# The sums of phi(k) on VectorE instead of TensorE, and roundings of landed inputs later in the written order

## The chip, the core and the metric

One core of a Trainium2 chip runs the kernel. Its engines work in parallel and wait for each other by semaphores: TensorE (PE, products; PEld is its loading of weights), VectorE (DVE), ScalarE (ACT), GpSimd (POOL) and SyncE (SP). SP and POOL issue most of the DMA transfers. The metric is the device time in microseconds of one execution; the time before is the median of three runs.

## The reference

x is 2048 x 1024. Two branches are computed from it and mixed by a gate per row. Branch A is linear attention with 32 heads of 32, B a gated MLP with 3584 hidden columns:

```python
q, k, v = split(x @ wqkv)                       # 32 heads of 32
phi_q = concat(softmax(q @ w_phi), softmax(-(q @ w_phi)))     # 64 features; phi_k alike from k
kv = einsum("bhsf,bhsd->bhfd", phi_k, v)
z  = einsum("bhsf->bhf", phi_k)
o  = einsum("bhqf,bhfd->bhqd", phi_q, kv) / (einsum("bhqf,bhf->bhq", phi_q, z)[..., None] + 1e-6)
a  = o @ wo
b  = (gelu(x @ w_gate) * (x @ w_up)) @ w_down
g  = sigmoid((x * gate_w).sum(-1))
out = g * a + (1 - g) * b
```

## The kernel before

Everything is fp32. Products run on operands split in two parts: a rounded one ("high", line 117, on ScalarE, type fp32r) and the remainder ("low", line 120, on VectorE); three passes (high with high, high with low, low with high) make one product. Matrix products of large blocks use a scheme with seven products of half-size blocks instead of eight (`LEFT`, `RIGHT`, `INTO`), so a **unit** (one 256-column group of v, k, q, gate or up, over one half of the rows) is seven groups of twelve `MATMUL` of 128x512 on line 741, named after the bank they go to: a, p, c, a, a, c11 and b. Names in profile rows: `wgu`, `tyz` and `v` are the rounded weights of a unit, `x` and `s` the rounded parts of x and of its sums, `stage` the places where loads land, `h` results on their way out. In rows of the profile the buffer c11 reads as c.

Between groups, ScalarE copies one bank to another so that the next products accumulate on it: c<-b (line 758), c11<-a (line 762; read in rows as c<-a) and b<-a (line 769). A copy is short, but it stands in ScalarE's queue in the written order, with the roundings.

That order is not left to a scheduler. The body (lines 134 to 1318) is written under a manual schedule: **streams** (Python generators) each yield a request (engine, assumed length, when ready, due), and `run` picks, product by product, the next one to emit, keeping a clock of its own with assumed lengths (`PRODUCT` 2.73 us, `LAND` 5.0 us for a load, and so on). `step` emits a group of products and notes when it begins and ends on that clock; small products (**fillers**) are put in behind a group once their inputs are assumed to be there. On the chip each engine then works its queue strictly in the order that came out; where a landing is later than assumed, all behind it on that engine waits.

Stages: a first part with the folding of w_phi into the key and query weights (lines 517 and 949), the gates (line 920, one product with gate_w for each 128 rows of x, whose loads come from SP), then the units of v and k, with gate and up units among them. `features` works on the background for each of 32 pairs (half of rows, head group, half of the group): a transpose, softmax of k, rounding of phi(k) into `pts`, and then additions over row blocks on VectorE (line 1022) that leave a 128x128 block `z` in the tile `tails` (line 1025). `accumulate` puts in as a filler eight products phi(k)^T v (line 1037) and one product of `z` with a column of ones (line 1039), which sums over partitions. The 257 columns go by ScalarE (line 1049) and a POOL DMA that adds into `kv_parts` in HBM. `finish` reads them back, sums and writes `sums_of`, from which `attention` works for q. From 1665 us on a last stage makes the output (line 1439).

x changes twice under the running products: at `first_turn` the right operands go from the second half of the rows to the first, at `second_turn` back. `x_convert` rounds each landed piece (its loads are line 270). `weights` and `lower_weights` load and round the weights of a unit.

Of the kernel before, what the change touches and what calls it, by code (L numbers as in the profile page):

```python
# [8 lines left out]
F32 = mybir.dt.float32  # L9
# [22 lines left out]
def tile_gated_mix(ctx: ExitStack, tc: tile.TileContext, x, xT, wkT, wqT, wv, w_phi, wo,  # L32
# [15 lines left out]
    one = keep.tile([P, 1], F32, name="one")  # L48
# [8 lines left out]
    kv_parts = dram.tile([P, H // 2, 2 * P + 1], F32, name="kvp")  # L57
# [76 lines left out]
    with tc.tile_pool(name="xa", bufs=1) as xa, tc.tile_pool(name="fp", bufs=1) as fp, \  # L134
# [16 lines left out]
        INF, PRODUCT, SIGNAL, LAND, STORE = 10.0 ** 9, 2.73, 0.12, 5.0, 4.5  # L151
        busy, begins, ends = {VEC: 0.0, SCA: 0.0}, {}, {}
# [119 lines left out]
        def x_convert(s, half, part, landed):  # L272
            i, j, last, need = part
            b0, s = 2 * half, s.rearrange("p (a b) -> p a b", a=2)
            end = yield SCA, 1.1, lambda: max(value(landed), done(last - 1)), need - 1.5
# [8 lines left out]
            low(q[1], s, q[0])  # L284
            return end

        def pieces(t, half, s, which, free, then=lambda end: None):
# [41 lines left out]
        def weights(n, half, kind, m):  # L329
# [4 lines left out]
            end = yield SCA, 1.1, lambda: max(landed, done(t - 9)), t - 2.2  # L334
# [28 lines left out]
        def lower_weights(n, kind, m, ke, e, ko, o, end, sums):  # L363
# [16 lines left out]
            end = yield SCA, 0.65, lambda: max(landed, done(t + 4)), t + 9.5  # L380
# [120 lines left out]
        nc.vector.memset(one, 1.0)  # L501
# [282 lines left out]
        def step(j, operand, *args, **kw):  # L784

            begins[j] = max(begins[j], operand - SIGNAL)
            product(*args, **kw)
# [49 lines left out]
        def last_products(n, half):  # L837
# [7 lines left out]
            mm=g_at.rearrange("p c q -> p (c q)")[:, :32], st=g_at.rearrange("p c q -> p (c q)")[:, 32:],  # L845
            z=tails[:, P:]))]
# [125 lines left out]
        def features(p):  # L972
# [12 lines left out]
            while job:  # L985
# [33 lines left out]
                end = yield VEC, 1.15, end - SIGNAL, soon()  # L1019
# [10 lines left out]
        v_free, z_free = [0.0], [0.0]  # L1030

        def accumulate(half, pair, pts, blocks):

            def emit_products(end):
                po = misc()
                for b in range(8):
                    nc.tensor.matmul(po[:, :2 * P], blocks[:, b], pts[:, b].rearrange("p e q f -> p (e q f)"),  # L1037
                                     start=b == 0, stop=b == 7, skip_group_check=True)
                nc.tensor.matmul(po[:, 2 * P:2 * P + 1], places[0].parts["z"], one, start=True, stop=True,
                                 skip_group_check=True)  # L1040
                misc_free[0] = INF
                pts_free[0] = v_free[0] = z_free[0] = end
# [3 lines left out]
        def accumulated(half, pair, po, end):  # L1046
            end = yield SCA, 0.45, lambda end=end: max(end, hidden_free()), now[0] + 2
            own = hidden()[:, :2 * P + 1]
            nc.scalar.activation(own, po[:, :2 * P + 1], AF.Copy)
# [5 lines left out]
        def finish(p):  # L1055
            landed = yield SYN, LAND + 7.0, lambda: max(max(kept), place_free(), v_free[0], pts_free[0]), INF
            zs, z = p.small("mm", 32)[:, :16], tails[:, :64]
# [4 lines left out]
            for c, t in enumerate(chunks):  # L1062
                nc.sync.dma_start(t.rearrange("p (u n) -> p u n", n=2 * P), kv_parts[:, 4 * c:4 * c + 4, :2 * P])
# [16 lines left out]
            yield VEC, 0.8, end - SIGNAL, soon()  # L1080
            nc.vector.memset(z[:, 16:32], 0.0)
            nc.vector.tensor_copy(z[:, :16], zs)
            nc.vector.transpose(z[:, 32:], z[:, :32])
# [444 lines left out]
```

## Time and profile before

| | |
|---|---|
| time, median of 3 | 2359.07 us (2357.88 to 2360.53) |
| profiled execution | 2356.42 us, its span 2354.4 us |
| TensorE busy | 2327.5 us, 99% of the span |
| VectorE, ScalarE busy | 1789.0 us, 1113.3 us |
| granted TensorE clock, mean | 0.996 |
| DMA | 622.36 MB, mean 264 GB/s |

In rows of a timeline stand the start and the length in us, the engine, line, operation, tiles (out<-in), shape and count, and in brackets the idle time of that engine ahead of it and what ended it. Lengths of neighbouring products overlap, since they are pipelined: the distance of two starts is the time a group takes. Rows of groups have total busy us, mean ns of one, and the idle time ahead. Rows of waits have the total, the count and the longest. Rows of stretches have from:to, length, then busy us and count of each engine shown (PE alone, or PE, PEld, DVE, ACT and POOL), the granted clock as a share of full speed, the DMA share and GB/s.

### The profile page before, as it was taken

What the parts mean: (1) busy time and instruction counts of PE and PEld (TensorE: products, weight loads), DVE (VectorE), ACT (ScalarE), POOL (GpSimd) and SP (SyncE); (2) the same over time, 40 slices, a digit from 0 to 9 for tenths busy, and PEclk for the clock granted to TensorE, in tenths of its full rate; (3) what the DMA queues carried; (4) which work ended last, traced back from release to release, by engine and by line L of the source; (5) the groups of instructions that cost most, each with busy time, mean ns of one, the idle gap of its engine ahead of it and who ended that gap; (6) DMA issues with size and microseconds to landing.
All of it is one profiled execution on the core that took longest, in us unless ns stands there. A gap on an engine that the chain in (4) does not pass through costs nothing.

```text
span 2354.4 us, 29380 instructions
## 1 busy us (share of the span) xinstructions
PE 2327.5 (99%) x10472; PEld 1930.8 (82%) x10472; DVE 1789.0 (76%) x2335; ACT 1113.3 (47%) x1498; POOL 379.0 (16%) x646
## 2 busy tenths in 40 slices
PE   8999999999999999999999999999999999999999
PEld 7777887888888888878888888888888888888887
DVE  6665787888888878866988888887574868767773
ACT  6435444555555555544565655655433222323221
POOL 3211111121222112122232222222000000000000
PEclk9999999999999999999999999999999999999999
DMA  9987447898989888899888888887784767978774
GB/s 340 308 295 275 146 155 257 307 314 289 324 304 308 309 282 295 284 294 256 246 257 247 235 248 250 236 249 239 263 286 157 260 237 264 322 258 316 262 268 136
DMA packets 242210, 622.36 MB, mean 264 GB/s; under 512 B 34000, under 2 KB 73680, under 8 KB 226192
## 3 DMA queue, kind: packets, MB, share of 16 engines
q1 hardware_dynamic: 152960, 308.48, 40.7%
q0 software_dynamic: 87904, 311.75, 39.6%
q8 instruction: 83, 1.36, 0.2%
q14 instruction: 63, 0.52, 0.1%
q10 hardware_dynamic: 1200, 0.26, 0.1%
HBM read 413.80 MB, written 206.59 MB: 264 GB/s over the span
## 4 chain that ended last, share of the span: by engine, by line
PE 90%; DMA 4%; issue 2%; DVE 2%; SPq 1%; ACT 1%; POOL 0%; DVEq 0%; ACTq 0%; POOLq 0%
PE po L1439 29%; PE a L741 25%; PE c L741 17%; PE b L741 8%; PE p L741 8%; PE misc L1194 1%; PE misc L1037 1%; DMA stage<-wk 1%; DMA stage<-in_wv 1%; DMA xs<-x 1%; SPq L968 1%; PE misc L949 0%; DMA stage<-in_xT 0%; DMA x<-in_xT 0%; DMA wk<-wgu 0%
## 5 line engine op out<-in xcount | busy, mean ns | idle before, releaser
L1439 PE MATMUL po<-tw,wgu 128*128 128x512 f32 x1344 | 309.8, 389 | 0.0
L1439 PEld LDWEIGHTS po<-tw,wgu 128*128 128x128 f32 x1344 | 252.3, 188 | 52.3
L117 ACT ACTIVATE wgu<-stage 128x1024 fp32r<-128x1024 f32 x130 | 137.5, 1058 | 301.5 <-PE po L1439 226.7
L120 DVE TENSOR_TENSOR wgu<-stage,wgu 128x1024 fp32r<-128x1024 f32 x130 | 158.8, 1221 | 131.1 <-ACT wgu L117 131.1
L741 PE MATMUL c<-x,tyz 128*128 128x512 f32 x948 | 234.5, 397 | 12.8 <-ACT c L758 10.9
L741 PE MATMUL c<-x,wgu 128*128 128x512 f32 x948 | 229.6, 391 | 0.3 <-ACT c L762 0.3
L741 PE MATMUL a<-s,tyz 128*128 128x512 f32 x948 | 229.6, 391 | 0.2 <-DVE tyz L120 0.2
L741 PE MATMUL b<-s,tyz 128*128 128x512 f32 x948 | 228.8, 390 | 0.0
L741 PE MATMUL a<-x,wgu 128*128 128x512 f32 x948 | 228.5, 390 | 0.3 <-DVE h L725 0.3
L741 PE MATMUL a<-s,v 128*128 128x512 f32 x948 | 228.8, 390 | 0.0
L741 PE MATMUL p<-s,tyz 128*128 128x512 f32 x948 | 228.2, 389 | 0.0
L741 PEld LDWEIGHTS c<-x,tyz 128*128 128x128 f32 x948 | 181.2, 192 | 53.7 <-ACT c L758 13.2
L741 PEld LDWEIGHTS a<-x,wgu 128*128 128x128 f32 x948 | 177.6, 188 | 37.8 <-DVE h L725 0.7
L741 PEld LDWEIGHTS a<-s,tyz 128*128 128x128 f32 x948 | 177.5, 188 | 37.7 <-DVE tyz L120 0.9
L741 PEld LDWEIGHTS p<-s,tyz 128*128 128x128 f32 x948 | 177.7, 188 | 36.7
L741 PEld LDWEIGHTS a<-s,v 128*128 128x128 f32 x948 | 177.4, 188 | 37.0 <-DMA v<-ru13v 0.3
L741 PEld LDWEIGHTS c<-x,wgu 128*128 128x128 f32 x948 | 177.0, 188 | 37.3 <-ACT c L762 0.7
L741 PEld LDWEIGHTS b<-s,tyz 128*128 128x128 f32 x948 | 177.4, 188 | 36.7
L1439 PE MATMUL po<-tw,wl 128*128 128x512 f32 x672 | 156.9, 389 | 0.0
L1439 PE MATMUL po<-tyz,wgu 128*128 128x512 f32 x672 | 155.2, 389 | 0.0
L1439 PEld LDWEIGHTS po<-tyz,wgu 128*128 128x128 f32 x672 | 126.2, 188 | 26.2
L1439 PEld LDWEIGHTS po<-tw,wl 128*128 128x128 f32 x672 | 126.2, 188 | 26.2
(440 smaller groups left out, 3556.2 us busy)
## 6 DMA issues: line engine op xcount, KB each, us to landing
stage<-lm SPq DMA_DIRECT2D x98, 512.0 KB, 3.7
sr<-in_w_down SPq DMA_DIRECT2D x84, 512.0 KB, 6.0
sl<-lm SPq DMA_DIRECT2D x70, 512.0 KB, 4.5
lm<-h POOLq DMA_DIRECT2D x112, 256.0 KB, 4.7
stage<-in_w_gate SPq DMA_DIRECT2D x28, 512.0 KB, 5.4
stage<-in_w_up SPq DMA_DIRECT2D x28, 512.0 KB, 6.5
stage<-la SPq DMA_DIRECT2D x28, 512.0 KB, 5.2
sr<-in_wo SPq DMA_DIRECT2D x20, 512.0 KB, 6.2
```

Of the source, the lines that this page charges most:

```text
L117: nc.scalar.activation(dst, src, AF.Copy)
L120: nc.vector.tensor_tensor(dst, src, dst_h.bitcast(F32), OP.subtract)
L741: nc.tensor.matmul(dst, w[:, h, 4 * part + kc, :], xq[:, e, kc, :], start=first and kc == 0 and i == 0, stop=kc == 3 and i == 2, skip_grou ...
L968: nc.sync.dma_start(into[64 * j + 32 * i:64 * j + 32 * i + 32, n], heads[k][half][g][j][64 * w:64 * w + 64, 256 * i:256 * i + 256] .rearra ...
L1037: nc.tensor.matmul(po[:, :2 * P], blocks[:, b], pts[:, b].rearrange("p e q f -> p (e q f)"), start=b == 0, stop=b == 7, skip_group_check=True)
L1194: nc.tensor.matmul(po[s], kbs[:, s].rearrange("p a b -> p (a b)"), pts[:, q, s, :], start=q == 0, stop=q == 1)
L1439: nc.tensor.matmul(ps[c], ls[:, a, m, c * P:(c + 1) * P], rs[:, e, m], start=opens and m == 0 and j == 0, stop=closes and m == 1 and j == 2)
```

## The change

1. **z.** The product with ones goes, and with it the column 257 of `kv_parts`. `features` puts the accumulation in as a filler before the additions, and after them transposes the 128x128 block in its 32x32 squares on VectorE and reduces it over 32 columns into four numbers per partition, kept in `tails` (`z_sums`). `finish` adds up the two halves of rows and the partition groups by additions and shifting copies on VectorE, transposes once, and starts the four DMAs of z to `sums_of` ahead of the summing of kv, not behind it. The fetch of z from HBM goes.
2. **Roundings.** `soft` lets the planner assume that a landed input is ready for its rounding up to 2 us later (`SPARE`) than the load lands, if its due time allows, from `first_turn` on. It holds for pieces of x, for the even weights of a unit and for its `v`.
3. **Other assumed times.** `step` takes the end of the roundings of its x pieces into account (`x_ready`); loads of x pieces have a due time; the landing of wqT is assumed 4 us later; VectorE's lengths are taken 2% shorter from some way behind `first_turn` and 5% (was 3%) behind `second_turn`; the filler of an accumulation is assumed 0.9 us long (was 1.1).

```diff
+        SPARE = 2.0
+        def soft(landed, due):
+            at = begins.get(now[0], INF)
+            if now[0] < first_turn:
+                return landed
+            return max(landed, min(landed + SPARE, (at if at < INF else 0.0) + (due - 1.5 - now[0]) * PRODUCT))
...
-            return request[1] * (0.97 if request[0] == VEC and now[0] > second_turn + 14 else 1.0) + (1.3 if len(request) > 4 and request[4] != table[0] else 0.0)
+            return request[1] * (1.0 if request[0] != VEC else 0.95 if now[0] > second_turn + 14 else 0.98 if now[0] > first_turn + 70 else 1.0) + (1.3 if len(request) > 4 and request[4] != table[0] else 0.0)
...
-            end = yield SCA, 1.1, lambda: max(value(landed), done(last - 1)), need - 1.5
+            end = yield SCA, 1.1, lambda: max(soft(landed, need - 1.5), done(last - 1)), need - 1.5
...
+        def x_ready(n, half, i):
+            if 7 * n < first_turn:
+                return 0.0
+            assert len(x_made[half, i]) == 2
+            return max(x_made[half, i])
...
-                landed = yield SYN, LAND + 3.5, lambda: max(begun(part[2] - 5), value(free)), INF
+                landed = yield SYN, LAND + 3.5, lambda: max(begun(part[2] - 5), value(free)), part[3] - 5
...
-            end = yield SCA, 1.1, lambda: max(landed, done(t - 9)), t - 2.2
+            end = yield SCA, 1.1, lambda: max(soft(landed, t - 2.2), done(t - 9)), t - 2.2
...
-            end = yield SCA, 0.65, lambda: max(landed, done(t + 4)), t + 9.5
+            end = yield SCA, 0.65, lambda: max(soft(landed, t + 9.5), done(t + 4)), t + 9.5
...
-            begins[j] = max(begins[j], operand - SIGNAL)
+            begins[j] = max(begins[j], operand - SIGNAL, x_ready(n, half, x) - SIGNAL)
...
-                landed = yield SYN, LAND + 2.0, lambda: free[g % 2], INF
+                landed = yield SYN, LAND + 6.0, lambda: free[g % 2], INF
                 nc.sync.dma_start(s, wqT[g])
...
-                end = yield VEC, 1.15, end - SIGNAL, soon()
+                fillers.append((lambda end=end: max(end, misc_free[0]), accumulate(half, 2 * g + w, pts, blocks), 0.9))
+                yield VEC, 1.15, end - SIGNAL, soon()
                 half_sums = p.wide[0].rearrange("p (q n) -> p q n", q=4)
...
-                end = yield VEC, 0.3, lambda: max(end, z_free[0]), soon()
-                z_free[0] = INF
-                nc.vector.tensor_tensor(p.parts["z"].rearrange("p (q f) -> p q f", q=4), half_sums[:, :, :32],
+                p.free = yield VEC, 0.7, 0.0, soon()
+                z, zt = p.wide[0][:, P:2 * P], p.wide[0][:, 3 * P:4 * P]
+                nc.vector.tensor_tensor(z.rearrange("p (q f) -> p q f", q=4), half_sums[:, :, :32],
                                         half_sums[:, :, 32:64], OP.add)
-                p.free = end
-                fillers.append((lambda end=end: max(end, misc_free[0]), accumulate(half, 2 * g + w, pts, blocks), 1.1))
+                nc.vector.transpose(zt, z)
+                nc.vector.tensor_reduce(z_sums[:, half, :, 2 * g + w], zt.rearrange("p (q t) -> p q t", q=4), AX.X, OP.add)
...
-                nc.tensor.matmul(po[:, 2 * P:2 * P + 1], places[0].parts["z"], one, start=True, stop=True,
-                                 skip_group_check=True)
...
-            nc.sync.dma_start(zs, kv_parts[:, :, 2 * P])
             soon = lambda: now[0] + 3
+            yield VEC, 1.1, 0.0, soon()
+            nc.vector.tensor_tensor(z, z, other, OP.add)
+            for at in (32, 96):
+                nc.vector.tensor_copy(other[at - 32:at], z[at:at + 32])
+            nc.vector.tensor_tensor(z[:96], z[:96], other[:96], OP.add)
+            nc.vector.tensor_copy(other[:32], z[64:96])
+            nc.vector.tensor_tensor(z[:32], z[:32], other[:32], OP.add)
+            nc.vector.transpose(other[:32], z[:32])
+            for q in range(4):
+                nc.gpsimd.dma_start(sums_of[32 * q:32 * q + 32, 1].rearrange("b u d -> u b d"),
+                                    other[16 * (q % 2):16 * (q % 2) + 16, 32 * (q // 2):32 * (q // 2) + 32]
+                                    .unsqueeze(1).to_broadcast([16, 32, 32]))
```

What the written order makes of it is seen in three places. In the changed file the lines have other numbers: the rounding is L116, c<-b L772, c<-a L776, b<-a L783, the gelu L711, the exponentials L1020, the products L755, the folds of the query weights L962, the remainder L119 and the copies of kv's sums L1103.

ScalarE, the first gate unit behind the key and value units, from the copy b<-a to the copy c<-b. Before:

```order
L769 ACTIVATE b<-a 128x512
L117 ACTIVATE tyz<-stage 128x1024
L117 ACTIVATE f<-x_374 128x16x32
L1049 ACTIVATE h<-misc 128x257
L780 ACTIVATE x_374<-p 128x512
L117 ACTIVATE v<-stage 128x512
L697 ACT_TABLE_LOAD
L697 ACTIVATE x_374<-c_349 128x512
L1007 ACT_TABLE_LOAD
L1007 ACTIVATE x_374<-x_374 128x512 x2
L758 ACTIVATE c<-b 128x512
L117 ACTIVATE tyz<-stage 128x1024
```

Now:

```order
L783 ACTIVATE b<-a 128x512
L116 ACTIVATE tyz<-stage 128x1024
L794 ACTIVATE x_373<-p 128x512
L1062 ACTIVATE h<-misc 128x256
L711 ACT_TABLE_LOAD
L711 ACTIVATE x_373<-c_348 128x512
L116 ACTIVATE v<-stage 128x512
L772 ACTIVATE c<-b 128x512
L116 ACTIVATE tyz<-stage 128x1024
L116 ACTIVATE f<-x_373 128x16x32
L116 ACTIVATE wgu<-stage 128x1024
```

The rounding of `v`, which waits for a load, was followed by a table load, the gelu, another table load and two exponentials before c<-b; now the gelu stands ahead of `v`, and c<-b directly behind it.

TensorE, the first four folds of the query weights (`misc<-f,raw`) among the groups of two units. Before:

```order
L741 MATMUL c<-x_398,tyz 128x512 x12
L949 MATMUL misc<-f,raw 128x128 x8
L741 MATMUL a<-s_340,tyz 128x512 x12
L741 MATMUL a<-s_342,v 128x512 x12
L949 MATMUL misc<-f,raw 128x128 x8
L741 MATMUL c_349<-x_396,wgu 128x512 x12
L741 MATMUL b<-s_341,tyz 128x512 x12
L741 MATMUL a<-x_395,wgu 128x512 x12
L741 MATMUL p<-s_339,tyz 128x512 x12
```

Now (the same stretch and the unit behind it, to the fourth fold):

```order
L755 MATMUL a<-s_339,tyz 128x512 x12
L962 MATMUL misc<-f,raw 128x128 x8
L755 MATMUL a<-s_341,v 128x512 x12
L755 MATMUL c_348<-x_394,wgu 128x512 x12
L755 MATMUL b<-s_340,tyz 128x512 x12
L962 MATMUL misc<-f,raw 128x128 x8
...
L962 MATMUL misc<-f,raw 128x128 x8
L755 MATMUL a<-s_341,v 128x512 x12
L755 MATMUL c_348<-x_394,wgu 128x512 x12
L755 MATMUL b<-s_340,tyz 128x512 x12
L755 MATMUL a<-x_393,wgu 128x512 x12
L962 MATMUL misc<-f,raw 128x128 x8
```

Before, the second fold of a unit stood right behind a<-s,v, in both units; now it stands two and then three groups later.

ScalarE, the second turn of x (`x01` is the piece that the product c<-x,tyz reads). Before:

```order
L723 ACTIVATE h_8221<-c11_349 128x512
L117 ACTIVATE x01_8226<-stage_8148 128x1024
L117 ACTIVATE x01_8226<-stage_8167 128x1024
L758 ACTIVATE c_351<-b_350 128x512
L762 ACTIVATE c11_349<-a_8219 128x512
```

Now:

```order
L737 ACTIVATE h_8294<-c11_348 128x512
L116 ACTIVATE x01_8299<-stage_8236 128x1024
L772 ACTIVATE c_350<-b_349 128x512
L116 ACTIVATE x01_8299<-stage_8253 128x1024
L776 ACTIVATE c11_348<-a_8292 128x512
```

One of the two roundings of `x01` moved behind c<-b. The two copies of kv's sums (`f<-x00 32x1024`, L1079, now L1103) moved up by more than a unit, from behind these rows to the c<-b before.

More of the change, by code (lines that the diff above doesn't have):

```diff
@@ L47, in tile_gated_mix @@
     pair_mask = keep.tile([P, 2, 32], F32, name="pair_mask")
-    one = keep.tile([P, 1], F32, name="one")
     logit = keep.tile([P, S // P], F32, name="logit")
@@ L56, in tile_gated_mix @@
     wq_fold = [dram.tile([P, KC * P], F32, name=f"wq{g}") for g in range(NG)]
-    kv_parts = dram.tile([P, H // 2, 2 * P + 1], F32, name="kvp")
+    kv_parts = dram.tile([P, H // 2, 2 * P], F32, name="kvp")
     xb = {}
@@ L284, in x_convert @@
             low(q[1], s, q[0])
+            x_made[half, i].append(end)
             return end
+        x_made = {(half, i): [] for half in range(2) for i in range(7)}
+        def x_ready(n, half, i):
[3 more added lines that the diff above has]
+            return max(x_made[half, i])
         def pieces(t, half, s, which, free, then=lambda end: None):
@@ L500, in tile_gated_mix @@
             nc.vector.memset(pair_mask[32 * j:32 * j + 32, j % 2, :], 1.0)
-        nc.vector.memset(one, 1.0)
         bd = fp.tile([P, NG, 4, 32], F32, tag="v", name="bd", bufs=1)
@@ L782, in banks, with step @@
                         yield from result(kind, half, m, 1, 0, c11, None, lambda: done(t + 5), t + 8)
-        def step(j, operand, *args, **kw):
-            begins[j] = max(begins[j], operand - SIGNAL)
-            product(*args, **kw)
+        def step(j, operand, n, dst, right, part, x, half, first=False):
+            begins[j] = max(begins[j], operand - SIGNAL, x_ready(n, half, x) - SIGNAL)
+            product(n, dst, right, part, x, half, first)
             ends[j] = begins[j] + PRODUCT
@@ L844, in tile_gated_mix @@
         places = [Place(work[:, 2048:3072], dict(
-            mm=g_at.rearrange("p c q -> p (c q)")[:, :32], st=g_at.rearrange("p c q -> p (c q)")[:, 32:],
-            z=tails[:, P:]))]
+            mm=g_at.rearrange("p c q -> p (c q)")[:, :32], st=g_at.rearrange("p c q -> p (c q)")[:, 32:]))]
         misc_free, other_free, SOON = [0.0], [0.0], 2
@@ L1038, in emit_products @@
                                      start=b == 0, stop=b == 7, skip_group_check=True)
-                nc.tensor.matmul(po[:, 2 * P:2 * P + 1], places[0].parts["z"], one, start=True, stop=True,
-                                 skip_group_check=True)
                 misc_free[0] = INF
-                pts_free[0] = v_free[0] = z_free[0] = end
+                pts_free[0] = v_free[0] = end
                 start(accumulated(half, pair, po, end + 0.25))
@@ L1047, in accumulated @@
             end = yield SCA, 0.45, lambda end=end: max(end, hidden_free()), now[0] + 2
-            own = hidden()[:, :2 * P + 1]
-            nc.scalar.activation(own, po[:, :2 * P + 1], AF.Copy)
+            own = hidden()[:, :2 * P]
+            nc.scalar.activation(own, po[:, :2 * P], AF.Copy)
             nc.gpsimd.dma_start(kv_parts[:, pair], own, **({} if half else dict(accum_op=OP.add)))
@@ L1056, in finish @@
             landed = yield SYN, LAND + 7.0, lambda: max(max(kept), place_free(), v_free[0], pts_free[0]), INF
-            zs, z = p.small("mm", 32)[:, :16], tails[:, :64]
+            z, other = tails[:, :64], tails[:, 64:P]
             p.second(new_f(F32)[:, :1024])
@@ L1079, in finish @@
                 nc.scalar.activation(p.wide[1][rows[h]], p.wide[0][64 * h + 32:64 * h + 64], AF.Copy)
[L1080 to L1083, printed above, removed]
-            for q in range(4):
-                nc.gpsimd.dma_start(sums_of[32 * q:32 * q + 32, 1].rearrange("b u d -> u b d"),
-                                    z[32 * q:32 * q + 16, 32:].unsqueeze(1).to_broadcast([16, 32, 32]))
             end = yield VEC, 2.5, moved, soon()
```

5 lines of the change are left out of this document (3 added, 2 removed).

## The prediction

> **What bounds the kernel now.** I read the page's busy line, then whom TensorE waited for, then its busy time and granted clock by stage, then the timeline at each wait.
>
> ```profile
> span 2354.4 us, 29380 instructions
> PE 2327.5 (99%) x10472; PEld 1930.8 (82%) x10472; DVE 1789.0 (76%) x2335; ACT 1113.3 (47%) x1498; POOL 379.0 (16%) x646
> ...
> PE c L741 <- ACT c L758: 10.9, 5, 3.9
> PE misc L949 <- issue: 3.0, 1, 3.0
> ...
> PE c L741 <- DVE x L120: 1.2, 1, 1.2
> PE c L741 <- ACT x L117: 0.7, 1, 0.7
> ...
> 60.00:150.00 90.00, 82.86 (x390) 1.00 0.87 297
> 150.00:235.00 85.00, 83.07 (x393) 0.96 0.83 286
> 403.00:1037.00 634.00, 634.00 (x2916) 528.87 (x2915) 525.26 (x672) 352.50 (x489) 124.68 (x220) 1.00 0.88 301
> 1049.00:1665.00 616.00, 616.00 (x2719) 1.00 0.84 244
> ```
> TensorE (PE) sets the time: from 403 to 1037 us and from 1049 to 1665 us its busy time equals the stretch. So two things count: products that leave its queue, and its few waits, which lie before 1049 us. In the waits a row gives the sum, the number of waits and the longest; in the stretches the third figure from the end is the granted clock.
>
> **Term 1, the z products.** Each of the 32 accumulations (eight products of line 1037) is followed by a one-column fp32 product (L1039, two passes), which goes.
>
> ```profile
> 275.74 1.12 PE L1037 MATMUL misc<-pts,f 128*128 128x256 f32 x8
> 276.69 0.28 PE L1039 MATMUL misc<-one,tails 128*128 128x1 f32 x2
> 276.83 3.03 PE L741 MATMUL a<-s,v 128*128 128x512 f32 x12
> 279.70 2.88 PE L741 MATMUL c<-x,wgu 128*128 128x512 f32 x12
> 282.42 2.88 PE L741 MATMUL b<-s,tyz 128*128 128x512 f32 x12
> ```
> By starts, a plain group of twelve takes 282.42 - 279.70 = 2.72 us; z with the group behind it takes 279.70 - 276.69 = 3.01. Each z costs 0.29 us, of which 0.14 is its own and 0.15 a slower group behind it. 32 x 0.29 = 9.3 us, on an engine without a pause there. If the slower group came from the eight products and stayed, 32 x 0.14 = 4.5. I take -9.3.
>
> **Term 2, the wait at 392 us.**
>
> ```profile
> 389.26 2.88 PE L741 MATMUL p<-s,tyz 128*128 128x512 f32 x12
> 396.04 5.49 PE L741 MATMUL c<-x,tyz 128*128 128x512 f32 x12 [3.90 <-ACT c L758]
> 401.33 3.19 PE L741 MATMUL a<-s,tyz 128*128 128x512 f32 x12
> 404.35 2.88 PE L741 MATMUL a<-s,v 128*128 128x512 f32 x12
> ...
> 390.50 0.63 ACT L117 ACTIVATE v<-stage 128x512 fp32r<-128x512 f32 x1 [6.43 <-DMA stage<-in_w_gate]
> 391.15 1.28 ACT L697 ACT_TABLE_LOAD   x1
> 392.45 0.60 ACT L697 ACTIVATE x<-c 128x512 f32<-128x512 f32 x1
> 393.06 1.28 ACT L1007 ACT_TABLE_LOAD   x1
> 394.36 1.15 ACT L1007 ACTIVATE x<-x 128x512 f32<-128x512 f32 x2
> 395.41 0.58 ACT L758 ACTIVATE c<-b 128x512 f32<-128x512 f32 x1
> ```
> The copy c<-b that the product needs stands on ScalarE behind the rounding of v, whose load landed late, and behind two table loads, a gelu and two exponentials. 404.35 - 389.26 = 15.09 us for three groups instead of 8.16: 6.9 us lost, of which 3.9 is idle and the rest half clock. In the changed order table load and gelu stand ahead of v, and c<-b directly behind it. Landing as late, the copy would begin at 391.15 and end at 391.73, before the 391.98 at which the product is due. -6.9; if the load comes 3.9 us later still, 0.
>
> **Term 3, the wait at 1040 us.**
>
> ```profile
> 1037.88 2.88 PE L741 MATMUL p<-s,tyz 128*128 128x512 f32 x12
> 1043.91 4.44 PE L741 MATMUL c<-x,tyz 128*128 128x512 f32 x12 [3.14 <-ACT c L758]
> 1048.19 2.89 PE L741 MATMUL a<-s,tyz 128*128 128x512 f32 x12
> ...
> 1042.32 1.06 ACT L117 ACTIVATE x<-stage 128x1024 fp32r<-128x1024 f32 x1 [3.94 <-DMA stage<-in_xT]
> 1043.28 0.58 ACT L758 ACTIVATE c<-b 128x512 f32<-128x512 f32 x1
> ```
> 1048.19 - 1037.88 = 10.31 for two groups instead of 5.44: 4.9 us. Two roundings of x stand ahead of c<-b; now one does. But the second half of the same product reads the second x: landing at 1042.32 as before, rounded and its remainder taken, it would still hold the product for over 2 us. What may bring it sooner is SP's queue: the four kvp reads of the sum (2 MB), which stood right ahead of these two x loads, now have ten other loads between, and the fetch of z in 4-byte pieces goes. Ends 0 and -4.9; I take the middle, -2.5.
>
> **Term 4, the wait at 146 us.**
>
> ```profile
> 149.45 3.56 PE L949 MATMUL misc<-f,raw 128*128 128x128 f32 x16 [2.97 <-issue]
> ...
> 147.91 1.22 DVE L920 SCALAR_TENSOR_TENSOR x<-x 128x1024 f32<-128x1024 f32 x1 [2.29 <-DMA x<-in_x]
> ...
> 149.06 0.28 DVE L459 TENSOR_TENSOR f<-f 128x128 f32<-128x128 f32 x1
> ...
> 153.70 1.22 DVE L920 SCALAR_TENSOR_TENSOR x<-x 128x1024 f32<-128x1024 f32 x1
> ...
> 231.00:236.00 5.00, 5.00 (x16) 3.95 (x15) 2.94 (x4) 1.72 (x2) 0.00 (x0) 0.66 0.98 298
> ```
> The product of line 949 needs the small mask product of L459, which stands on VectorE (DVE) behind a gate product waiting for its x rows. 2.97 us idle, and then half clock: after the shorter waits at 228 us (0.7 and 1.2 idle) the five us from 231 ran at a mean 0.66, 1.7 us lost, and I price this one alike: 4.7. In the changed order this fourth fold stands three groups later: due at 149.45 - 2.97 + 8.16 = 154.6. On DVE its mask now follows the ninth gate product instead of the seventh. At the old pace the ninth began at 153.70; with the product, a half remainder (0.6) and the mask (0.3) that makes 155.8, a wait of some 1.2 us instead of 2.97 and its half clock. I take -3.5; ends -4.7 and 0, the latter if the x rows come 2 us later still.
>
> The Trainium skill (TensorE: Matmul & The Clock Gate, HAM oscillation) tells of no harm from PE gaps under about 3.4 us. By it only term 2 holds half clock, and terms 3 and 4 shrink by 0.9 and 1.7. The trace differs: the 0.66 followed idles of 0.7 and 1.2 us.
>
> **Term 5, what is late next.**
>
> ```profile
> 136.20 3.04 PE L741 MATMUL c<-x,tyz 128*128 128x512 f32 x12 [2.05 <-ACT c L758]
> L120 DVE TENSOR_TENSOR wgu<-stage,wgu 128x1024 fp32r<-128x1024 f32 x130 | 158.8, 1221 | 131.1 <-ACT wgu L117 131.1
> ```
> Here c<-b stands behind a rounding of wgu that waits for its load, and still does: ahead of x's first turn the softening does not act. That load stands on SP's queue behind the fourth load of gate rows, which needs the buffer of the second gate product; that product now stands behind one remainder (1.2 us) and two half-size sums (as much again). Up to 2.5 us later, or nothing if the load lands sooner for less traffic: +1.0, ends -3.7 (2.05 and half clock gone) and +2.5. The waits at 228 us (1.9 idle, 1.7 by clock) have roundings of x behind one of wgu before and after: 0, ends -3.6 and +2.
>
> For the new order as a whole I add one new wait of the size seen at 228 us, 0.7 idle and 1.7 by clock: +2.4. Its likeliest place is the second turn, where the two copies of the attention sums, which need the kvp reads, eight additions and a transpose, now stand on ScalarE ahead of an h<-c and a c<-b; they stood behind both. Ends 0 and +7, the price of term 2. More would be at odds with the rows: the old order had no wait in 403 to 1037 and 1049 to 1665, 1250 us, and in the new one a rounding of wgu stands between copy b<-a and copy c<-b in 6 of 79 places instead of 30.
>
> **Hidden parts.** z's sum on DVE:
>
> ```profile
> L988 DVE STREAM_TRANSPOSE x<-x 128x1024 f32<-128x1024 f32 x32 | 39.8, 1245 | 1.1
> L1083 DVE STREAM_TRANSPOSE tails<-tails 128x32 f32<-128x32 f32 x1 | 0.2, 213 | 0.0
> L995 DVE TENSOR_REDUCE g_at<-x 128x16 f32<-128x512 f32 x32 | 21.7, 678 | 0.1
> ```
> A transpose of 128 columns lies between 213 and 1245 ns, in proportion near 0.31 us; the reduction of 128 below 0.68, near 0.28. 32 x 0.59 = 19 us more on DVE, which idles 109 of the 634 us to 1037: nothing on PE's path; uncovered, 19. The accumulation is now queued for PE ahead of these sums, so it does not wait for them. At the end ten small operations replace three and the four stores of sums on POOL's queue come earlier; PE has products from the other stream there: 0, at most 2 if DVE is late. The spills shrink from 257 to 256 columns: 0. ScalarE issues the same copies.
>
> **Sum.** -9.3 - 6.9 - 2.5 - 3.5 + 1.0 + 2.4 = -18.8. It is made against the profiled execution, 2356.4 us (2 us around its span); the runs shown have their median 2.7 us higher, 2359.07. I take the change from there: 2340.
>
> **Rivals.** (a) The new order waits elsewhere: the gain of z stays, the waits removed come back at other landings, net -4.5 to -12, about 2350. For it: each wait came from one late landing (ScalarE stood 6.4 us for v's load), and every order has such. Against: 403 to 1037 without one. (b) All of the waits go, and nothing new comes: -9.3 - 6.9 - 4.9 - 4.7 - 3.6 - 3.7 = -33, about 2326. (c) Slower: VectorE falls behind its written order. The planner now takes 2% and 5% off its durations while z's sums add 0.59 us per pair; the remainders of wgu and tyz that PE reads come late, once per unit. Each such wait would cost as at 228 us, 3.6; from six on (21.6) they eat the gain, at nine (one in four of some 38 units) the time is 2359 - 19 + 32 = 2372. Against: DVE ended but 1.2 us of PE's waits after 60 us, above. The Trainium skill (VectorE: DVE Perf Modes, Rules for kernel authors) calls the reduction DVE's slowest operation and advises to restructure; the row's 678 ns for 512 columns agrees, and by it (c) is where the move would go wrong. (d) The change does nothing: z's load and passes hide under their neighbours. The 3.01 against 2.72 speaks against it.
>
> **How the numbers follow.** Forecast 0.62 (own range 2332 to 2348), (a) 0.18, (b) 0.09, (c) 0.07, (d) 0.04. The range leaves out (c), (d) and the far ends of (a) and (b): 2328 to 2352. A measurement here tells apart about 0.2%, 4.7 us: faster the forecast, (b) and nearly all of (a), 0.88; same (d) and a rest of (a), 0.06; slower 0.06.
>
> **What would show it.** No group at the z line and a plain 2.72 us behind each accumulation; PE waits for c<-b near 392 us gone; the L949 wait gone or down to about 1.2; at the second turn a wait of 0 to 2.5 us that names x, not c; at 136 us one of 2 to 4.5. Wrong, if PE's idle time before 1049 us is not at least 5 us less, or if waits for DVE appear between 403 and 1665.

## The result, and the profile after

The changed kernel takes 2339.31 us (median of 5 runs, 2337.32 to 2343.70), the kernel before beside it 2359.07; the ratio is 0.9929, 95% interval 0.9907 to 0.9952. Predicted were 2340, and 2328 to 2352. The time is right; of the six terms of its sum the first two hold in size, and the others went otherwise.

The page's busy line, and the waits of TensorE, of the changed kernel:

```profile
span 2339.3 us, 29314 instructions
PE 2315.9 (99%) x10408; PEld 1921.2 (82%) x10408; DVE 1811.5 (77%) x2402; ACT 1111.0 (47%) x1496; POOL 380.2 (16%) x646
...
PE misc L962 <- issue: 3.9, 1, 3.9
PE c L755 <- ACT c L772: 3.4, 3, 2.7
PE b L755 <- ACT b L783: 2.3, 2, 1.8
```

The copy c<-b, which TensorE awaited for 10.9 us, now costs 3.4; a wait for b<-a (L783) is new, and the wait for a fold (L962) has grown from 3.0 to 3.9. VectorE has 22 us more, TensorE 11.6 less.

For a reckoning by stage I took from both traces, for each group of products, the distance from its start to the next group's start, less that of the same pair where nothing disturbs it. What is left is time lost, idle or at a lower clock. Two profiled executions of the kernel before are shown (the second is an experiment below).

```
us lost in     0-60  60-245  245-440  440-1000  1000-1065  1065-end   all
before          8.2    14.5      7.0       0.2        4.9       0.2  34.9
before again    8.0    16.7      4.6       0.1        7.1       0.7  37.0
changed         7.8    15.6      0.0       0.0        4.6       0.0  28.2
```

So 7 to 9 us less are lost: against the first execution nearly all of it at one place, 245 to 440 us, against the second 4.6 there and 2.5 at the second turn. With 8.3 us for the products of z (next) this is 15 to 17 us, the difference of the profiled spans (2354.4 and 2356.5 against 2339.3). The medians shown lie 20 apart: single executions of the kernel before range widely, in 66 beside the experiments from 2346.85 to 2364.65, with medians of 2354 to 2359 from one set of executions to the next. The ratio's interval, 11 to 22 us, holds both.

**z.** TensorE's timeline at an accumulation, changed kernel:

```profile
282.90 1.12 PE L1052 MATMUL misc<-pts,f 128*128 128x256 f32 x8
283.86 2.91 PE L755 MATMUL b<-s,tyz 128*128 128x512 f32 x12
286.60 2.88 PE L755 MATMUL a<-x,wgu 128*128 128x512 f32 x12
```

From the accumulation to the group behind the next it is 286.60 - 282.90 = 3.70 us; before, 279.70 - 275.74 = 3.96, and so at all 32 places of both traces. 0.26 us each, 8.3 in all.

**The gate unit at 392 us.** ScalarE's and SP's timelines, changed kernel:

```profile
385.85 0.60 ACT L711 ACTIVATE x<-c 128x512 f32<-128x512 f32 x1
386.35 0.62 ACT L116 ACTIVATE v<-stage 128x512 fp32r<-128x512 f32 x1
386.96 0.58 ACT L772 ACTIVATE c<-b 128x512 f32<-128x512 f32 x1
...
370.35 0.91 SPq L43 DMA_DIRECT2D stage<-in_w_gate  x2
384.73 2.41 SPq L981 DMA_DIRECT2D x<-v  x4
```

c<-b stands right behind v, and ends at 387.5; the product that needs it starts at 392. But v was not late here at all: there is no idle time ahead of its rounding. In the kernel before, SP issued all three loads of in_w_gate behind the fetches of v and k:

```profile
377.88 3.26 SPq L968 DMA_DIRECT2D x<-v  x4
381.19 4.55 SPq L968 DMA_DIRECT2D x<-k  x4
385.79 6.43 SPq L43 DMA_DIRECT2D stage<-in_w_gate  x3
```

So the order on SP moved too, two of the loads by 15 us, v's own (the first of them) included. By these lengths either move alone would have ended the wait. For the load the record bears this out: in the changed kernel without the later roundings (an experiment below), v's load is issued at 375.3 us, ahead of the fetches of v and k, and a table load, the gelu and a rounding of wgu still stand between the rounding of v and c<-b. ScalarE's v and TensorE's product, that run:

```profile
385.28 0.63 ACT L116 ACTIVATE v<-stage 128x512 fp32r<-128x512 f32 x1
...
393.92 2.88 PE L755 MATMUL c<-x,tyz 128*128 128x512 f32 x12
```

Neither row has idle time ahead of it, and c<-b ends there at 389.2. So this wait goes without the later roundings; whether c<-b directly behind a late v would have sufficed, no run shows.

**Up to 245 us.** The waits at 136 and 149 us are gone, and others are there. TensorE, VectorE, and then stretches (the third figure from the end is the granted clock), changed kernel:

```profile
111.51 3.04 PE L755 MATMUL c<-x,tyz 128*128 128x512 f32 x12 [2.72 <-ACT c L772]
172.06 3.65 PE L962 MATMUL misc<-f,raw 128*128 128x128 f32 x16 [3.87 <-issue]
...
170.34 0.69 DVE L97 TENSOR_TENSOR stage<-stage 128x512 f32<-128x512 f32 x1 [5.59 <-DMA stage<-wk]
...
171.68 0.28 DVE L474 TENSOR_TENSOR f<-f 128x128 f32<-128x128 f32 x1
...
172.00:176.00 4.00, 3.94 (x18) 3.90 (x19) 3.96 (x6) 1.33 (x2) 0.00 (x0) 0.57 0.38 122
```

The mask (L474) of a later fold stands behind sums of two halves of wk (L97, L98), and these wait 5.6 us for a load: 3.9 us idle and half clock behind it.

**The second turn.** TensorE, ScalarE and SP, changed kernel:

```profile
1017.40 1.43 PE L755 MATMUL c<-x,wgu 128*128 128x512 f32 x5 [0.61 <-DVE x L119]
1020.66 4.30 PE L755 MATMUL b<-s,tyz 128*128 128x512 f32 x12 [1.84 <-ACT b L783]
...
1017.05 1.06 ACT L116 ACTIVATE s<-stage 128x1024 fp32r<-128x1024 f32 x1 [0.96 <-DMA stage<-xs]
1019.07 1.06 ACT L116 ACTIVATE s<-stage 128x1024 fp32r<-128x1024 f32 x1 [0.96 <-DMA stage<-xs]
1020.03 0.58 ACT L783 ACTIVATE b<-a 128x512 f32<-128x512 f32 x1
...
1002.03 6.54 SPq L1108 DMA_DIRECT2D sums<-f  x3
...
1011.65 0.82 SPq L276 DMA_DIRECT2D stage<-xs  x2
```

On SP the stores of sums, four in a row up to 1008.6 us (the row shows three), and one load of in_xT stand ahead of the two loads of xs, which are issued at 1011.7 and 1012.1; the roundings that wait for them begin 5.4 and 7.0 us later. (The expectations below speak of an issue of in_xT of 5.1 us: that row is two issues of 0.38 us each with SP's own waiting between them, and it lies behind these loads of xs.) The wait has moved from c<-b behind roundings of x01 to b<-a behind two roundings of s, some 20 us earlier, at nearly the same price.

### The profile page after: what moved, and what is told of

Its sections match the earlier page's. It is cut to its first block, busy times and chain, and to the rows that moved or that the text cites. A ratio compares the mean times of both kernels' runs of the same rounds, so it can differ in the third digit from the quotient of the medians.

```text
span 2339.3 us, 29314 instructions
## 1 busy us (share of the span) xinstructions
PE 2315.9 (99%) x10408; PEld 1921.2 (82%) x10408; DVE 1811.5 (77%) x2402; ACT 1111.0 (47%) x1496; POOL 380.2 (16%) x646
## 4 chain that ended last, share of the span: by engine, by line
PE 92%; DMA 4%; issue 2%; DVE 1%; ACT 1%; POOL 0%; SPq 0%; DVEq 0%; POOLq 0%; ACTq 0%
PE po L1456 29%; PE a L755 25%; PE c L755 17%; PE b L755 9%; PE p L755 8%; PE misc L1052 1%; PE misc L1211 1%; DMA stage<-wk 1%; DMA raw<-in_xT 1%; DMA stage<-in_wv 1%; DMA x<-in_xT 0%; PE misc L962 0%; DMA stage<-xs 0%; DMA wk<-stage 0%; DMA xs<-x 0%
## 5 line engine op out<-in xcount | busy, mean ns | idle before, releaser
L116 ACT ACTIVATE wgu<-stage 128x1024 fp32r<-128x1024 f32 x130 | 137.5, 1058 | 305.2 <-PE po L1456 227.8
L119 DVE TENSOR_TENSOR wgu<-stage,wgu 128x1024 fp32r<-128x1024 f32 x130 | 158.6, 1220 | 127.8 <-ACT wgu L116 127.7
L755 PE MATMUL c<-x,tyz 128*128 128x512 f32 x948 | 228.8, 390 | 4.1 <-ACT c L772 3.4
L755 PE MATMUL b<-s,tyz 128*128 128x512 f32 x948 | 229.6, 391 | 2.3 <-ACT b L783 2.3
L755 PE MATMUL a<-s,v 128*128 128x512 f32 x948 | 228.3, 389 | 1.5 <-DVE s L119 0.8
L755 PE MATMUL c<-x,wgu 128*128 128x512 f32 x948 | 228.7, 390 | 0.9 <-DVE x L119 0.6
L755 PE MATMUL a<-x,wgu 128*128 128x512 f32 x948 | 228.6, 390 | 0.8 <-DVE h L739 0.8
L755 PE MATMUL a<-s,tyz 128*128 128x512 f32 x948 | 228.4, 389 | 0.2 <-DVE tyz L119 0.2
L755 PE MATMUL p<-s,tyz 128*128 128x512 f32 x948 | 228.1, 389 | 0.0
L755 PEld LDWEIGHTS c<-x,tyz 128*128 128x128 f32 x948 | 177.3, 188 | 42.6 <-ACT c L772 5.0
L755 PEld LDWEIGHTS b<-s,tyz 128*128 128x128 f32 x948 | 178.0, 189 | 39.8 <-ACT b L783 3.1
L755 PEld LDWEIGHTS a<-s,v 128*128 128x128 f32 x948 | 177.8, 188 | 38.9 <-ACT s L116 1.2
L755 PEld LDWEIGHTS a<-x,wgu 128*128 128x128 f32 x948 | 178.1, 188 | 38.5 <-DVE h L739 1.2
L755 PEld LDWEIGHTS c<-x,wgu 128*128 128x128 f32 x948 | 177.1, 188 | 37.9 <-DVE x L119 1.0
L755 PEld LDWEIGHTS a<-s,tyz 128*128 128x128 f32 x948 | 177.4, 188 | 37.0 <-DVE tyz L119 0.7
L755 PEld LDWEIGHTS p<-s,tyz 128*128 128x128 f32 x948 | 177.4, 188 | 36.4
```

Of the source, the lines that this page charges most:

```text
L116: nc.scalar.activation(dst, src, AF.Copy)
L119: nc.vector.tensor_tensor(dst, src, dst_h.bitcast(F32), OP.subtract)
L755: nc.tensor.matmul(dst, w[:, h, 4 * part + kc, :], xq[:, e, kc, :], start=first and kc == 0 and i == 0, stop=kc == 3 and i == 2, skip_grou ...
```

## The experiments

Theory: the gain is z's 8.3 us plus the wait at 392 us; the latter went because roundings of landed inputs come later in the written order (part 2 of the change, called the softening below). Rivals: z alone makes it; the later roundings alone make it; z's own price is smaller. Ratios are to the kernel before, run on the same chip.

**The product put back.** The order of all else stays as it is.

```diff
+        nc.vector.memset(tails[:, P:], 1.0)
...
+                nc.tensor.matmul(po[:, 2 * P:2 * P + 1], tails[:, P:], tails[:, P:P + 1], start=True, stop=True,
+                                 skip_group_check=True)
```

> The changed kernel with the one-column fp32 product put back behind each of the 32 accumulations (it multiplies a constant block, nobody waits for its result, and the written order of every other instruction stays the same). Theory: the product left TensorE's path at 0.25 to 0.29 us each, its own 0.14 and a slower group behind it, so it comes back as 8 to 9.3 us: some 2347.5 to 2348.5 us, no new wait, and the group behind it 3.0 from the start of the one-column product to the next plain group. Rival 1: only its own passes count, 32 x 0.14 = 4.5 us: 2344. Rival 2: its load and passes hide under their neighbours, and the gain came from the waits alone: 2339 to 2340.

2345.2 us, 0.9954 (0.9938 to 0.9970): 5.9 us more than the changed kernel, below the theory's 8 and above rival 1's 4.5. The intervals, 4 to 5 us either way, tell neither from it; the trace does. TensorE's timeline:

```profile
284.41 1.12 PE L1053 MATMUL misc<-pts,f 128*128 128x256 f32 x8
285.36 0.28 PE L1055 MATMUL misc<-tails 128*128 128x1 f32 x2
285.50 2.97 PE L756 MATMUL b<-s,tyz 128*128 128x512 f32 x12
288.32 2.88 PE L756 MATMUL a<-x,wgu 128*128 128x512 f32 x12
```

288.32 - 284.41 = 3.91, against 3.70 without: 0.21 each, 6.6 in all. It has no wait over 1 us in 245 to 1000 either. The product does cost more than its own 0.14, but in this form 0.05 less than the one that was removed, whose operand was the fresh z and not a constant, and whose column was in another tile. Which of the two makes the difference was not tried.

**The two parts, alone and together.** z alone (part 2 and part 3 taken back, but for the filler's 0.9 us, which goes with z):

```diff
-        SPARE = 2.0
+        SPARE = 0.0
```

with the lengths, the wait for x's roundings, the due time of x pieces and the landing of wqT as before. The next two have the softening alone, on the kernel before; and z with the softening, without the rest of part 3.

> The change of z without the later roundings and the other assumed times. Theory: 8.2 us for the product; the wait at 392 us stays in part, since in this order a table load, the gelu and the rounding of a wgu still stand between the rounding of v and the copy c<-b: 0.63 + 1.28 + 0.60 + 1.1 + 0.58 us behind a load that lands at 390.5 would end at 394.7 against 392 due, a wait of 2 to 3 us and half clock, 4 to 5 us of the 6.9; the fold waits at 149 us and the second turn stays as before, 4.7 and 4.9. Together 2359 - 8.2 - 2.5 = 2348, between 2345 and 2352. Rival 1: z alone makes the whole gain: 2340. Rival 2: the load of v lands elsewhere in this order and all waits change: more than 2353 or less than 2343.

> The kernel before with the softening alone: z stays on TensorE, all other assumed times as before. It completes the square of the two parts (neither 1, z alone 0.9989, both 0.992). Theory: in this order no copy c<-b stands behind two exponentials and a late v any more, so the wait at 392 us is gone (5 to 7 us); z still costs 0.26 us at each of 32 places, and other late landings (the tyz whose sums VectorE makes, which are not softened) may cost 2 to 5 us between 440 and 1000 us, as in the run of all times without z: 0.996 to 0.999. Rival: the softening brings 18 us by itself, as its removal from the changed kernel cost 18: 0.9935 or less.

> The change of z and the softening alone: VectorE's lengths, the landing of wqT, the due time of x pieces and the wait for x's roundings are those of the kernel before. Theory: these two carry the gain together, since without the softening the order with z on VectorE has new waits for c<-b (z alone 0.9989 of the kernel before, all without the softening 0.9997); no wait over 1 us between 245 and 1010 us, the fold wait at 149 us and waits at both turns as before, 0.993 to 0.996 of the kernel before. Rival: the softening needs one of the other assumed times, and waits for c<-b or b<-a stay in 245 to 1010 us: 0.997 or more.

```
                  without z's move            with z's move
no softening      1                           0.9989 (0.9977 to 1.000)
softening         0.9970 (0.9958 to 0.9981)   0.9920 (0.9903 to 0.9937)
```

z alone was predicted at 2348 and took 2355.74: its second rival. Softening alone, 2349.71, lies in the theory's range, though not a wait was left in 440 to 1000 us where I had allowed for 2 to 5. Both together, 2336.8, are a little better than the theory, and as fast as the changed kernel within the intervals. By sums the two would give 0.9959; they give 0.9920, some 9 us more (4 to 15, estimated from the three intervals). Why, shows the time lost, each row from one execution (3.2 us over its kernel's median, 3.7 under and 3.4 over, so that a few us between rows mean nothing):

```
us lost in      0-60  60-245  245-440  440-1000  1000-1065  1065-end
z alone          8.7    19.4      0.0      12.3        4.2       1.1
softening alone  9.3    12.4      0.0       0.1        2.9       0.1
both             7.7    18.5      0.0       0.0        0.6       0.4
```

The move of z changes what the planner does everywhere behind it. Without the softening new waits arise where there were none. Two of them, z alone: ScalarE and TensorE at 458 us, VectorE and TensorE at 494 us.

```profile
456.43 1.06 ACT L116 ACTIVATE wgu<-stage 128x1024 fp32r<-128x1024 f32 x1 [7.18 <-DMA stage<-in_w_gate]
457.39 0.58 ACT L772 ACTIVATE c<-b 128x512 f32<-128x512 f32 x1
458.02 4.26 PE L755 MATMUL c<-x,tyz 128*128 128x512 f32 x12 [1.98 <-ACT c L772]
...
491.01 0.69 DVE L97 TENSOR_TENSOR stage<-stage 128x512 f32<-128x512 f32 x1 [3.88 <-DMA stage<-in_w_up]
...
492.35 1.22 DVE L119 TENSOR_TENSOR pts<-x,pts 128x1024 fp32r<-128x1024 f32 x1
493.62 2.08 PE L1052 MATMUL misc<-pts,f 128*128 128x256 f32 x8 [2.75 <-DVE pts L119]
```

The 12.3 us that they and their like cost eat z's 8.3, though nothing is lost at 392 us here either. This is what the prediction's rival (a) describes, and it came true in the order without softening, at a higher price: by the medians 2.8 us are gained, where (a) had 4.5 to 12.

**All but the softening, and all but z.** The changed kernel with SPARE 0; and the kernel before with parts 2 and 3 (the filler stays at 1.1 us there).

> The changed kernel with the softening at 0 us instead of 2 us. Theory: it is the softening that took the rounding of v and of wgu from ahead of c<-b; without it a table load, the gelu and a rounding of wgu stand between v and c<-b at the first gate unit, and the wait near 392 us comes back with 2 to 3 us idle and half clock: 2339.3 + 4 to 7 = 2343 to 2346. Rival 1: the 392 wait went for another reason (the accumulation's length, VectorE's lengths), and the time stays 2339. Rival 2: the order without it is worse at many c<-b copies (a rounding of wgu stands ahead in most units): over 2350.

> The kernel before with the later roundings and the other assumed times, z still on TensorE. Theory: the 6.9 us of the wait at 392 us go (c<-b stands right behind v), the rest stays about even (fold wait gone at 149 us and back at 172 us, both turns the same): 2359 - 7 = 2352, between 2349 and 2355, and 32 groups at the z line as before. Rival 1: the gain of the change is all z's, and this is 2359. Rival 2: in this order, too, another copy comes to stand behind a late load: 2356 to 2362.

Without the softening 2357.28, 0.9997 (0.9985 to 1.001): nothing of the gain is left, and the theory's 2343 to 2346 was far off; its second rival came true. The wait at 392 us did not come back, as shown above. The kernel loses 3.9 us in 245 to 440 and 18.7 in 440 to 1000. At 499 us stands the very row of events that the kernel before had at 392 us (a rounding of v that waited for its load, then two table loads, the gelu and the exponentials, then c<-b), on ScalarE, and TensorE's product behind:

```profile
494.10 0.63 ACT L116 ACTIVATE v<-stage 128x512 fp32r<-128x512 f32 x1 [4.68 <-DMA stage<-in_w_gate]
...
497.96 1.15 ACT L1020 ACTIVATE x<-x 128x512 f32<-128x512 f32 x2
499.01 0.58 ACT L772 ACTIVATE c<-b 128x512 f32<-128x512 f32 x1
499.64 4.60 PE L755 MATMUL c<-x,tyz 128*128 128x512 f32 x12 [3.24 <-ACT c L772]
```

What the softening does to the order can be counted in ScalarE's rows of the traces: a rounding of wgu stands between b<-a and c<-b at 6 of 79 places in the changed kernel, and likewise with both parts alone, with the softening alone and with all but z; at 30 in the kernel before, at 38 with z alone and at 39 here.

All but z took 2354.91 (one of its twelve executions took 8426 us), 0.9985 (0.9974 to 0.9996), at the edge of the theory's range; what its second rival names is what happened. Its 4.8 us lost in 440 to 1000 are two waits for b<-a behind the rounding of a tyz, which the softening does not reach; the first of them:

```profile
666.95 1.06 ACT L117 ACTIVATE tyz<-stage 128x1024 fp32r<-128x1024 f32 x1 [4.08 <-PE c L757]
...
668.54 3.01 PE L757 MATMUL b<-s,tyz 128*128 128x512 f32 x12 [1.63 <-ACT b L785]
```

**VectorE's lengths, and more softening.** The changed kernel with VectorE's lengths as before; and with the softening at 4 us.

> The changed kernel with VectorE's assumed lengths as in the kernel before (1.0, and 0.97 behind the second turn). It tells whether the shorter lengths cost (rival c of the prediction) or pay. Theory: TensorE waited for VectorE for 3 us in all in the changed kernel, so the lengths decide little by themselves; z stays gone (8.3 us) and c<-b stays directly behind v, 2337 to 2343. Rival c: the shorter lengths make VectorE late and cost; without them 2335 or less. Rival: the lengths are part of what keeps the late landings out of the way, as the softening is (18 us): 2345 to 2357, with waits for c<-b between 400 and 1000 us.

> The changed kernel with the softening at 4 us instead of 2 us. Theory: the late landings between 240 and 1010 us are covered by 2 us already (no wait there), so 4 us gains at most at the second turn, where b<-a stands behind two roundings of s whose load landed 2 us late (1.8 us idle and 1.5 to 2 by half clock): 2335 to 2339. Rival: roundings that come 2 us later still reach TensorE late themselves, and waits for remainders (VectorE) appear between 240 and 1010 us: 2342 to 2355.

2341.96, 0.9946 (0.9925 to 0.9967), and 2341.22, 0.9945 (0.9924 to 0.9965): both as the changed kernel within the intervals, about 5 us either way. Neither loses over 0.3 us in 245 to 1000. By that the lengths are no part of the gain, and rival (c) of the prediction has nothing for it here. With 4 us the second turn loses 0.9 instead of 4.6, but a wait of 3.7 us for the remainder of s appears at the first turn, and the start, which the edit does not touch, happened to lose 2.8 us more.

**The losses up to 245 us.** The mask asked for before its load has landed; and the softening from the start on.

```diff
-                end = yield VEC, 0.3, landed, now[0] + 6
+                end = yield VEC, 0.3, 0.0, now[0] + 6
...
-            if now[0] < first_turn:
-                return landed
```

> The changed kernel with the small mask product of the query folds asked for before its wqT load has landed (it does not read that load), so that it no longer stands on VectorE behind the sums of wk that wait for their load; the fold itself still waits for both. Theory: the wait of 3.9 us at 172 us came from the place of the mask; it goes with its 1.5 us or so of half clock, 4 to 5.5 us: 2334 to 2336. Rival 1: the fold waits for the load of wqT itself, and the wait stays: 2339. Rival 2: the gate products, which move by a few places, make other waits between 140 and 240 us: 2339 to 2343.

> The changed kernel with the softening from the start on, not from x's first turn on. Theory: the wait of 2.7 us at 111 us is a copy c<-b behind the rounding of a wgu that waits for its load, of the kind that the softening takes away later; it goes, and the smaller ones at 70, 90 and 160 us with it: 2 to 4 us, 2335 to 2337. Rival: before the turn the loads come later than 2 us behind their assumed time (SP's queue is full of gate rows), the rounding stands in another copy's way or the remainder reaches TensorE late: 2339 to 2343.

2342.25, 0.9948 (0.9927 to 0.9968), and 2338.91, 0.9934 (0.9911 to 0.9957): no gain from either, as rival 2 of the first and the rival of the second had it. The wait at 172 us is gone with the early mask, and the wait at 111 us with the early softening, but in 60 to 245 us they lose 17.3 and 18.1, against 15.6. With the early mask TensorE waits 2.1 us for h (L739) at 154 us. The rows are of the early softening, where x's own sums stand on VectorE ahead of a remainder:

```profile
75.74 0.69 DVE L236 TENSOR_TENSOR raw<-raw 128x512 f32<-128x512 f32 x1 [7.25 <-DMA raw<-in_xT]
76.35 1.22 DVE L119 TENSOR_TENSOR tyz<-stage,tyz 128x1024 fp32r<-128x1024 f32 x1
77.62 3.98 PE L753 MATMUL a<-s,tyz 128*128 128x512 f32 x10 [3.59 <-DVE tyz L119]
```

In all these runs the loss up to 245 us is 21 to 28 us, and no edit tried lowered it beyond what executions of one kernel differ by.

**The second turn.** The kvp reads wait for the loads of x.

```diff
-            landed = yield SYN, LAND + 7.0, lambda: max(max(kept), place_free(), v_free[0], pts_free[0]), INF
+            landed = yield SYN, LAND + 7.0, lambda: max(max(kept), place_free(), v_free[0], pts_free[0], begun(second_turn + 9)), INF
```

> The changed kernel with the four kvp reads of the sum (2 MB) issued only behind all loads of x's second turn on SP's queue. Theory: what is late at the second turn is the landing of xs and in_xT behind the kvp reads and the stores of sums (an issue of in_xT took 5.1 us there, xs landed 7 us after its issue); with these behind, b<-a is no longer late and the 4.6 us lost at 1015 to 1027 us go in great part: at most 1.5 us of waits between 1005 and 1060 us, 3 to 4.6 us faster than the changed kernel, 0.9910 to 0.9917 of the kernel before. Rival 1: the roundings come late by the ring's places, not by the queue, and the waits stay. Rival 2: the sums now come late for the attention of the next q unit, and TensorE waits between 1060 and 1200 us: no gain, or slower.

2338.42, 0.9930 (0.9916 to 0.9944). The loss in 1000 to 1065 us is 0.0 instead of 4.6: what the edit puts behind the x loads on SP's queue, the reads and with them the stores of sums, was the cause. The two loads of xs are issued from 1005.8 us on, 6 us sooner; in the changed kernel it was the stores that stood right ahead. But 1.5 us are lost anew in 440 to 1000 (the written order there is the same; the landings differ), and 2.2 behind 1570 us, where VectorE stood 7.9 us for the reading of the sums, now later, and then had the attention's work ahead of an addition (L729) that TensorE needs:

```profile
1572.65 0.36 DVE L1143 TENSOR_TENSOR x<-x,pair_mask 128x64 f32<-128x64 f32 x2 [7.93 <-DMA x<-sums]
...
1584.45 3.01 PE L755 MATMUL a<-x,wgu 128*128 128x512 f32 x12 [1.72 <-DVE h L729]
```

**The kernel before, once more.**

> The kernel before once more, unchanged, to see whether another execution waits at the same places. Theory: the waits follow from the written order, so the one near 392 us and the one near 1040 us come again, each within 2 us of 3.9 and 3.1 idle, and the lesser ones before 240 us vary; span 2345 to 2362. Rival: landings vary so much that the 392 us wait is absent or another copy of 242 to 1010 us waits over 2 us in its place.

2358.54 us. The two late waits are where they were, 2.6 and 4.3 us idle; those before 240 us vary.

```profile
384.84 8.04 SPq L43 DMA_DIRECT2D stage<-in_w_gate  x3
391.16 0.63 ACT L117 ACTIVATE v<-stage 128x512 fp32r<-128x512 f32 x1 [6.53 <-DMA stage<-in_w_gate]
396.70 4.61 PE L741 MATMUL c<-x,tyz 128*128 128x512 f32 x12 [2.64 <-ACT c L758]
1044.48 5.42 PE L741 MATMUL c<-x,tyz 128*128 128x512 f32 x12 [4.33 <-ACT c L758]
```

No version is faster than the changed kernel beyond the intervals; the lowest median is that of z with the softening alone.

## Why the prediction was right, point by point

- **Term 1 (-9.3): right in kind, 8.3 measured.** The group behind the accumulation is not quite plain (2.74 us), so 0.26 goes and not 0.29. The bound of 4.5 is refuted: a product put back costs 6.6 by its trace even with a constant block.
- **Term 2 (-6.9): the size is right (4.6 to 7.0 measured), its step only in part.** The wait is gone. I had the copy saved by ScalarE's order with the load landing as late as before; the load also came 15 us sooner on SP's queue, which I did not read for this place. That the size came out is thus luck in part. A late v does make such a wait in the old sequence, as the run without the softening shows at 499 us; but at 392 us v was not late, and there that run waits for nothing with a table load, the gelu and a rounding between v and c<-b. In that order the earlier load alone was enough. What brings it ahead of the fetches was not found: it stands there in the four kernels with 2 us of softening read at this place and in the one without it, and behind them with z alone and in both executions of the kernel before.
- **Term 3 (-2.5): wrong in kind, -0.3 to -2.5 measured.** I asked what the product of x01 would wait for, and not what now stood ahead of b<-a, 20 us sooner: two roundings of s. The hint at SP's queue was right, as the run with later kvp reads shows, but in the changed order these reads, and now the stores of sums too, still stood ahead of most x loads.
- **Term 4 (-3.5): wrong.** The fold at 149 us no longer waits, but the step looked at the fourth fold alone; a later mask came to stand behind two sums that wait for wk. The price named for one new wait (+2.4, placed at the second turn) was paid here. Together with term 5 the net up to 245 us, predicted at -0.1 with that new wait, is +0.7 against the first profile of before.
- **Term 5 (+1.0): wrong place.** The wait at 136 us went instead of growing, and that at 111 us, which I did not cost, grew from 1.44 to 2.72.
- **Hidden parts: right.** The transpose and the reduction take 312 and 288 ns (estimated at 310 and 280), 64 instructions, and nobody waits for them:

```profile
L1041 DVE STREAM_TRANSPOSE x<-x 128x128 f32<-128x128 f32 x32 | 10.0, 312 | 1.1
L1042 DVE TENSOR_REDUCE tails<-x 128x4 f32<-128x128 f32 x32 | 9.2, 288 | 1.1
```

- **Sum.** By traces it is -8.3 - 7.0 - 0.3 + 0.7, and -0.4 in the other stages: -15, where -18.8 was predicted; the medians differ by 19.8 because the profiled execution of before was 2.7 us under its median and that of after 1.9 over it. The agreement to 1 us is thus luck beyond what the working deserves.
- **Its own signs.** Two of those that were to mean wrong appeared. TensorE's idle time before 1049 us went from 23.0 us to 19.5, 3.4 less and not 5 (5.2 less than the second execution of before); and a wait for VectorE stands at 1017 us, 0.61 long. The fold's wait grew to 3.9, the one at the second turn names b more than x, and none is left at 136 us. The lost time fell by more than the idle time because less ran at a lower clock. So the total held, and the account of the waits did not.
- **Rivals.** (a) holds in kind for the order with z and without the softening, and for the stretch up to 245 us. (c) and (d) are refuted; against (c) I had given VectorE 1.2 us of the waits before, and with 0.3 for h (L725) at 128 us it was 1.5. What the prediction missed is that the two parts need each other: it added z and the later roundings as separate terms, while without the softening z's move brings 12 us of new waits. The Trainium skill's warning of the reduction (VectorE: DVE Perf Modes, Rules for kernel authors), weighed in (c), did not bite at 0.29 us for 128 columns. Nor do the 678 ns for 512 columns, which I read as agreeing with it, show the reduction as slower than others: an addition of 128x512 takes 0.69 us in the rows above. From the Trainium skill's rule against gaps longer than about 3.4 us (TensorE: Matmul & The Clock Gate, HAM oscillation) I took that shorter ones do no harm; the lower clock below, behind gaps of 0.61 and 1.84 us, does not agree.

## What to carry to other kernels

A written order is one thing: an edit that saves time on the bounding engine also reshuffles every queue, and its gain shows only if late landings stay clear of the copies that this engine needs. So when costing such an edit, read the issuing queue of each late load as well as the engine that waits, and look at the instructions that come to stand behind it one stage earlier and later. Where landings vary, assume them later when placing what depends on them alone, and compare parts alone and together before crediting either.

## What the runs showed of the hardware that was not expected

The half clock does not follow the length of the gap. In the changed kernel 2.72 us idle at 111 us left the next stretch at full clock, 0.7 and 0.8 at 237 us too, while 0.61 and 1.84 at 1017 to 1020 us were followed by a mean of 0.66, as in the kernel before 0.7 and 1.2 at 228 us. Stretches of the changed kernel:

```profile
111.00:115.00 4.00, 3.49 (x15) 2.89 (x16) 3.96 (x6) 2.33 (x4) 1.66 (x4) 1.00 0.92 367
...
235.00:241.00 6.00, 4.50 (x19) 3.21 (x18) 2.33 (x2) 3.00 (x4) 0.54 (x1) 1.00 0.43 134
1021.00:1026.00 5.00, 5.00 (x16) 3.94 (x15) 2.53 (x4) 2.97 (x5) 2.34 (x4) 0.66 0.73 224
```

What decides it stays open. And a one-column fp32 product among these groups costs more than its own passes: 0.26 us with a fresh operand and 0.21 with a constant one, of which 0.14 are its own.
